# Attention with a two-layer FFN on one core: which score tile goes first after a row-maximum block, and a plan made anew

## The chip, the cores and the metric

The kernel runs on one core of one Trainium2 chip. Its time is the device time of one execution in microseconds (us); lower is better. The kernel before took 840.44 us, the median of three runs (839.09 to 842.27). Three engines matter most here: TensorE (PE in the profile; PEld are its weight loads), VectorE (DVE) and ScalarE (ACT); GpSimd (POOL) adds, and SyncE (SP) issues transfers.

## The reference

Attention over 32 heads (4 x 8) with pairs of queries averaged, so 576 queries and 1152 keys of depth 64 per head; then an FFN on 2304 tokens of width 512, with an inner width of 2048:

```python
q_pool = q.reshape(B, H, S // 2, 2, D).mean(axis=3)
scores = scale * np.matmul(q_pool, k.transpose(0, 1, 3, 2))
scores = scores - np.max(scores, axis=-1, keepdims=True)
attn = np.exp(scores)
attn = attn / (np.sum(attn, axis=-1, keepdims=True) + 1e-09)
x = np.matmul(attn, v)                      # then heads side by side: 2304 x 512
h = x @ w_in
g = np.maximum(h, 0.0) + alpha * np.minimum(h, 0.0)
return g @ w_out
```

## The kernel before

The heads are worked on in 16 pairs. The two heads of a pair lie in the two 64-row halves of TensorE's array (`both`, line 635): head 0 of a pair is tile 0, head 1 tile 1. A matmul on one tile can run beside one on the other.

Three kinds of work of a pair go to the tiles. **Row maxima** (`pair_max`, line 792): q against k, 128 queries by 384 keys in one matmul (line 818), into one PSUM bank, and VectorE reduces the bank to a maximum per query (line 839). A pair has 24 such blocks and 4 short ones for the last 64 queries (two matmuls of line 825 each). The list runs through the tiles in turn, 0, 1, 0, 1. The maxima are turned (line 855) and stored as `mq`. **Scores** (`half_main`, line 934): for each half of the queries (288) and each of 9 blocks of 128 keys, eight matmuls, four for each tile: high by high, high by low and low by high parts of k and q, and a product that takes off the maximum. They are issued 0, 1, 0, 1, ... into two banks, one for each tile. ACT takes the exponential of each bank (line 968). **Weighted sums** (line 995): after nine blocks of a half, the exponentials against v, in both tiles' columns, all rows; no score or maximum runs beside them. Sums of the exponentials (lines 981 and 1017), the division and the store to DRAM follow in `pair_end`.

The FFN (`hidden`, `low_sweep`, `high_sweep`, all through line 479) uses weights that VectorE and ACT split into parts (`w_convert`, lines 399 to 438: lines 409, 415, 421, 427 and 391 on VectorE). Ten conversions have no later use than attention's end and are spread over it; the rest come later.

The order of all instructions is made when the program is built, by a planner (`Scheduler`, line 109). Each piece of work is given to `add` with its engine, a planned duration in ns, what it reads and writes, and a priority in units of heads. `run` steps through a planned time: on each engine it looks at what could start within a slack of the earliest start (SLP, SLA, SLD for TensorE, ACT, VectorE) and takes the lowest priority number. Planned durations are constants: 545 for a score block, 130 for a maximum block, 190 for a short one. PSUM banks are handed out by the planner as well: `share` (line 1104) gives lists of banks to scores, maxima and the FFN, EARLY first and LATE from the end of head 13 (SWITCH) on, and a taker gets the one that is planned to be free first. The parameters of `attention_ffn` are priorities, slacks and lists of this kind. Engines then run their queues in the planned order and wait for each other by semaphores.

Of the kernel before, what the change touches and what calls it, by code (L numbers as in the profile page):

```python
# [13 lines left out]
AF = mybir.ActivationFunctionType  # L14
# [94 lines left out]
class Scheduler:  # L109
# [3 lines left out]
    def __init__(self, col_cost, turn, to_pe, from_pe, slack, dma_fixed):  # L113
        self.tasks, self.ready = [], [[] for _ in range(5)]
        self.free = [0.0] * 5
        self.dma_free = 0.0
        self.now = 0.0
        self.col = 0
        self.lock_free = 0.0
        self.turn = turn  # L120
        self.col_cost, self.to_pe, self.from_pe, self.slack = col_cost, to_pe, from_pe, slack
        self.dma_fixed = dma_fixed
        self.hold = ()

    def add(self, eng, dur, emit, reads=(), writes=(), uses=(), deps=(), prio=0.0, col=0, size=0, kind=None, dma=False, lock=False, fixed=None):
        t = Task()
# [99 lines left out]
def attention_ffn(  # L226
# [8 lines left out]
    NLO: int = 5,  # L235
    PB: int = 13,
    QB: int = 2,
    DF: int = 1985,
    D0: int = 1153.836,
    AQ: int = 0,  # L240
    F0: float = 7.572,
    F2: float = 0.839,
    FD: tuple = (1, 1, 1),
    WE: float = 24.0,
    WG: int = 1,
    WT: float = 6.74,
    WM: int = 2,
    WB: int = 300,
    WN: int = 2,
    TO_PE: int = 89,  # L250
    FROM_PE: int = 40,
    SLP: int = 45,
    SLA: int = 48,
    SLD: int = 138,
    QL: float = -0.025,
    KL: float = 1.207,
    KR: float = 1.497,
    KS: float = 0.082,
    M0: float = 1.211,
    E0: float = 1.868,  # L260
    BD: int = 7,
    SD: tuple = (3, 20),
    LD: tuple = (0, 33),
    TD: tuple = (3, 33),
    SR: float = 0.311,
    KQ: float = 0.342,
    KKB: int = 2,
    FQ: int = 1,
    FB: tuple = (1, 7),
    SF: int = -39,  # L270
    Q0: float = -2.2,
    Q1: float = 2.605,
    GROUPS: tuple = ((8,), (8,)),
    PARTS: tuple = (((0, 1, 2), (3, 4), (5, 6), (7, 8)), ((0, 1, 2, 3), (4, 5, 6, 7, 8))),
    JH: int = 0,
    AB: int = 10,
    ADDS: tuple = ((4, 6, 8), (6, 8)),
    PL: int = 0,
    LV: int = -2,
    LW: int = -8,  # L280
    GSB: int = 1,
    YSB: int = 4,
    R0: float = 4.187,
    R1: float = -5.36,
    R2: float = -7.727,
    R3: float = -0.231,
    W0: float = 5.34,
    W1: float = 1.69,
    W2: float = 18.088,
    W3: float = 0.137,  # L290
    YL: float = 0.337,
    MS: float = 0.136,
    EARLY: tuple = ((1, 2, 3, 4, 6), (0, 5, 6), ()),
    LATE: tuple = ((0, 1, 2, 3, 4, 5, 6), (0, 1, 2, 3, 4, 5, 6), (1, 2, 3, 4, 5, 6)),
    SWITCH: int = 13,
    GL: float = 23.364,
    COL: float = 0.151,
    HW: float = -1.194,
    XB: int = 4,
    PT: int = 17,  # L300
    VB: int = 4,
# [4 lines left out]
    QA: float = 1.0,  # L306
    REUSE: int = 6,
    NW: tuple = (464, 460, 460, 460, 460),
    RP: float = 31.088,
    RS: float = -1.017,  # L310
    RM: int = 30,
    RATE: float = 342.662,
):
    nc = tc.nc
# [6 lines left out]
    HQ = SQ // 2  # L321
# [6 lines left out]
    SCALE = 0.5 / float(D) ** 0.5  # L328
# [20 lines left out]
    sch = Scheduler(COL, SF, TO_PE, FROM_PE, (SLP, SLA, SLD, 0, 0), DF)  # L349
# [285 lines left out]
    both = [slice(i * D, (i + 1) * D) for i in range(2)]  # L635
# [156 lines left out]
    def pair_max(n, w):  # L792
# [15 lines left out]
        for x, (t, j, i) in enumerate(items):  # L808
            ms, d = Buf(r_ms), both[i]
            p = n - M0 - 0.5 * MS * (len(items) - 1 - x)  # L810
            if first:
                p = -9 + 0.01 * x
            rest = t < 0
            m = S // 4 if rest else JW

            def rows(t=t, j=j, d=d, ms=ms):
                if t >= 0:
                    nc.tensor.matmul(  # L818
                        out=ms.t[:, :JW], lhsT=w.q1.t[d, starts[t]:starts[t] + P],
                        rhs=w.k1.t[d, j * JW:(j + 1) * JW], start=True, stop=True,  # L820
                    )
                    return
                for u in range(2):
                    c = (2 * j + u) * (S // 4)
                    nc.tensor.matmul(  # L825
                        out=ms.t[:, :S // 4], lhsT=w.rt.t[d, D - D * u:D - D * u + P],
                        rhs=w.k1.t[d, c:c + S // 4], start=u == 0, stop=u == 1,
                    )

            dur = 190 if rest else 130  # L830
            if first:
                deps = w.k_in if rest else [w.k_in[j], w.q_in[2 * (t > 1)]]
                add(PE, dur, rows, uses=[w.q1, w.k1], reads=[w.rt] if rest else (), deps=deps, writes=[ms], prio=p, kind="m", col=1)
# [19 lines left out]
        def turn():  # L853
# [9 lines left out]
            for i, d in enumerate(both)  # L863
# [4 lines left out]
                out=mm.t[:2, :D], in0=mt.t[1][:2, :D], in1=mm.t[:2, :D].bitcast(F32), op=ALU.max  # L868
# [65 lines left out]
    def half_main(n, h, w):  # L934
# [7 lines left out]
        for c in range(NC):  # L942
            s = slice(c * P, (c + 1) * P)
            p, ps = Buf(r_p), Buf(r_ps)
            at = n + h + c / NC

            def scores(ps=ps, s=s):
                pairs = ((w.k1, w.q1), (w.k1, w.q2), (w.k2, w.q1), (None, w.mq))
                for x, (k, r) in enumerate(pairs):
                    for i, d in enumerate(both):  # L950
                        nc.tensor.matmul(  # L951
                            out=ps.t[i][:, :HQ], lhsT=k.t[d, s] if k else neg[d], rhs=r.t[d, q],
                            start=x == 0, stop=x == len(pairs) - 1,
                        )
# [10 lines left out]
            for i in range(2):  # L965
                add(
                    ACT, act(HQ, True),
                    lambda ps=ps, p=p, i=i: nc.scalar.activation(  # L968
                        out=p.t[:, i], in_=ps.t[i][:, :HQ], func=AF.Exp, scale=SCALE
                    ),  # L970
                    reads=[ps], writes=[p], prio=at + 0.01 * i,
                )
# [261 lines left out]
```

## Time and profile before

| what | value |
|---|---|
| median of three runs | 840.44 us (839.09 to 842.27) |
| profiled execution | 839.95 us, of which the span 838.2 us |
| PE busy | 825.2 us (98%) |
| PEld busy | 691.4 us (82%) |
| DVE busy | 567.0 us (68%) |
| ACT busy | 437.4 us (52%) |
| POOL busy | 262.4 us (31%) |

The profile is of one execution. The span goes from the first instruction to the last. Busy times are of instructions in flight, so a tile of TensorE can stand still while the engine counts as busy. "out<-in" names the tiles that an instruction writes and reads: `bank` is a PSUM bank, `pa` the exponentials, `bx` the maxima of a block. Attention fills the time up to about 440 us, with FFN work beside it from about 385 us on; the rest is the FFN.

### The profile page before, as it was taken

To read this page: it belongs to the slowest core of one execution; us is meant where nothing else is said; L and a number is where in the kernel's file an instruction comes from. 1 tells how busy PE (TensorE), PEld (TensorE's weight loads), DVE (VectorE), ACT (ScalarE), POOL (GpSimd) and SP (SyncE) were. 2 spreads that over 40 slices of the span, in tenths; PEclk is the share of its full clock that TensorE was granted. 3 is DMA by queue.
4 is the path that set the end of the run, shared out by engine and by line. 5 is a ranking of instruction groups with operands and counts; after the bars stand their busy time and mean duration, and the time that the engine had idled before them with its cause. 6 is when DMAs were issued, how large, how long until landed. Compare 5 with 4: busy or idle time off the path is not lost.

```text
span 838.2 us, 17447 instructions
## 1 busy us (share of the span) xinstructions
PE 825.2 (98%) x6690; PEld 691.4 (82%) x6690; DVE 567.0 (68%) x1035; ACT 437.4 (52%) x1124; POOL 262.4 (31%) x196
## 2 busy tenths in 40 slices
PE   8999999999999999999999999999999999999997
PEld 8767777676777777776779999998898988988986
DVE  7999999999998988889963799632242232322422
ACT  4657676675766676665754676643232233332321
POOL 5665665565565665654550000000000000000000
PEclk9999999999999999999999999999999999999999
DMA  8234345634354433323233768581330421300301
GB/s 274 58 89 164 82 144 140 197 115 123 87 179 122 122 116 77 83 72 109 69 124 121 248 195 260 177 228 58 91 92 3 120 59 46 91 0 1 91 1 45
DMA packets 67759, 93.71 MB, mean 112 GB/s; under 512 B 20004, under 2 KB 45404, under 8 KB 67676
## 3 DMA queue, kind: packets, MB, share of 16 engines
q1 hardware_dynamic: 65516, 88.18, 33.9%
q0 software_dynamic: 2160, 4.42, 3.6%
q8 instruction: 52, 0.85, 0.4%
q14 instruction: 31, 0.25, 0.1%
HBM read 73.48 MB, written 19.02 MB: 110 GB/s over the span
## 4 chain that ended last, share of the span: by engine, by line
PE 86%; DVE 9%; DMA 2%; issue 1%; ACT 1%; SPq 0%; DVEq 0%; ACTq 0%
PE bank L479 44%; PE bank L951 18%; PE bank L995 15%; PE bank L818 6%; DVE bx L839 3%; PE bank L1017 2%; DMA wraw<-wt 1%; DVE x L1066 1%; DVE pa L981 1%; PE bank L825 1%; PE bank L1129 1%; DMA kk<-kt 1%; DVE pos L515 1%; DVE r L1054 0%; DVE wbits L415 0%
## 5 line engine op out<-in xcount | busy, mean ns | idle before, releaser
L981 POOL TENSOR_TENSOR pa<-pa,pa 128x576 f32<-128x576 f32 x160 | 240.5, 1520 | 155.9 <-ACT pa L968 104.4
L839 DVE TENSOR_REDUCE bx<-bank 128x1 f32<-128x384 f32 (+1 forms) x448 | 214.0, 533 | 22.5 <-PE bank L818 19.9
L968 ACT ACTIVATE pa<-bank 128x288 f32<-128x288 f32 x576 | 199.7, 417 | 25.9 <-PE bank L951 17.4
L951 PE MATMUL bank<-q,k 64*128 64x288 f32 x1728 | 206.2, 311 | 0.8 <-DVE mq L923 0.6
L951 PEld LDWEIGHTS bank<-q,k 64*128 64x128 f32 x1728 | 163.3, 184 | 21.1 <-issue 9.3
L995 PE MATMUL bank<-pa,vv 128*64 128x288 f32 x1152 | 146.8, 409 | 0.0
L995 PEld LDWEIGHTS bank<-pa,vv 128*64 128x64 f32 x1152 | 79.9, 137 | 54.8 <-issue 3.8
L526 DVE TENSOR_TENSOR gw<-gs,gw 128x460 fp32r<-128x460 f32 (+1 forms) x55 | 35.1, 638 | 121.2 <-ACT gw L521 121.2
L951 PE MATMUL bank<-mq,neg 64*128 64x288 f32 x576 | 115.2, 291 | 0.0
L818 PE MATMUL bank<-k,q 64*128 64x384 f32 x384 | 110.1, 362 | 3.5 <-DVE bx L839 2.0
L521 ACT ACTIVATE gw<-gs 128x460 fp32r<-128x460 f32 (+1 forms) x55 | 32.4, 589 | 126.7 <-PE bank L479 115.2
L479 PE MATMUL bank<-wlow,wh 128*128 128x460 f32 (+1 forms) x320 | 93.0, 371 | 0.0
L479 PE MATMUL bank<-gw,wh 128*128 128x460 f32 (+1 forms) x320 | 92.8, 371 | 0.0
L951 PEld LDWEIGHTS bank<-mq,neg 64*128 64x128 f32 x576 | 83.3, 184 | 0.0
L818 PEld LDWEIGHTS bank<-k,q 64*128 64x128 f32 x384 | 62.4, 185 | 16.2 <-DVE bx L839 10.0
L515 DVE SCALAR_TENSOR_TENSOR gs<-gs,nal 128x460 f32<-128x460 f32 (+1 forms) x55 | 38.4, 699 | 52.9 <-ACT gs L510 52.9
L479 PE MATMUL bank<-x,wlow 128*128 128x288 f32 x480 | 66.3, 296 | 0.0
L479 PEld LDWEIGHTS bank<-wlow,wh 128*128 128x128 f32 x320 | 60.0, 188 | 7.1
L479 PE MATMUL bank<-gs,wlow 128*128 128x288 f32 x480 | 65.8, 295 | 0.1
L479 PEld LDWEIGHTS bank<-gw,wh 128*128 128x128 f32 x320 | 60.1, 188 | 6.8
L479 PEld LDWEIGHTS bank<-x,wlow 128*128 128x128 f32 x480 | 64.2, 188 | 1.6 <-issue 1.4
L479 PEld LDWEIGHTS bank<-gs,wlow 128*128 128x128 f32 x480 | 63.9, 188 | 1.4 <-DVE gs L526 0.5
(90 smaller groups left out, 1006.2 us busy)
## 6 DMA issues: line engine op xcount, KB each, us to landing
wraw<-wt SPq DMA_DIRECT2D x32, 512.0 KB
vv<-vt SPq DMA_DIRECT2D x32, 288.0 KB
xs<-x SPq DMA_DIRECT2D x32, 288.0 KB
x<-xs SPq DMA_DIRECT2D x32, 288.0 KB
kk<-kt SPq DMA_DIRECT2D x15, 576.0 KB
r<-rrd SPq DMA_DIRECT2D x64, 72.0 KB
yp<-ys SPq DMA_DIRECT2D x32, 144.0 KB
wlow<-xs SPq DMA_DIRECT2D x16, 288.0 KB
```

The source lines that it names most:

```text
L479: nc.tensor.matmul(out=ps[:, :n], lhsT=w[a, c // DMO][:, c % DMO:c % DMO + P], rhs=lo(hl), start=(first and i == 0), stop=(last and i == 2),)
L515: lambda: nc.vector.scalar_tensor_tensor(out=flat(pos), in0=flat(neg), scalar=nal[:, f:f + 1], in1=flat(pos), op0=ALU.mult, op1=ALU.add),
L521: ACT, act(n), lambda: nc.scalar.activation(out=gs.t[:, 0, :n], in_=flat(pos), func=AF.Copy),
L526: lambda: nc.vector.tensor_tensor(out=gs.t[:, 1, :n], in0=flat(pos), in1=gs.t[:, 0, :n].bitcast(F32), op=ALU.subtract),
L818: nc.tensor.matmul(out=ms.t[:, :JW], lhsT=w.q1.t[d, starts[t]:starts[t] + P], rhs=w.k1.t[d, j * JW:(j + 1) * JW], start=True, stop=True,)
L825: nc.tensor.matmul(out=ms.t[:, :S // 4], lhsT=w.rt.t[d, D - D * u:D - D * u + P], rhs=w.k1.t[d, c:c + S // 4], start=u == 0, stop=u == 1,)
L839: nc.vector.tensor_reduce(out=bx.t[:, at, j:j + 1], in_=ms.t[:, :m], axis=AX.X, op=ALU.max)
L951: nc.tensor.matmul(out=ps.t[i][:, :HQ], lhsT=k.t[d, s] if k else neg[d], rhs=r.t[d, q], start=x == 0, stop=x == len(pairs) - 1,)
L968: lambda ps=ps, p=p, i=i: nc.scalar.activation(out=p.t[:, i], in_=ps.t[i][:, :HQ], func=AF.Exp, scale=SCALE),
L981: lambda a=a, b=p, part=part, e=e: e.tensor_tensor(out=part.t, in0=a.t, in1=b.t, op=ALU.add),
L995: nc.tensor.matmul(out=av.t[i * D:(i + 1) * D, :HQ], lhsT=w.vv[i].t[:, e], rhs=p.t[:, i], start=(e == 0), stop=(e == NC - 1),)
L1017: nc.tensor.matmul(out=ps.t[g * 32:(g + 1) * 32, :HQ], lhsT=ones, rhs=acc[n + g // 2][j].t[:, g % 2], start=j == 0, stop=j == m - 1, tile_ ...
```

## The change

The planner keeps in `sch.tile` the tile of the last block that was issued. A scores block looks at it when it is issued: if the last one ended on tile 0, the block issues tile 1 first, else tile 0 first, and notes the tile that it issues last. The two exponentials of the block follow in that order. Besides, the planned times of maximum blocks become 165 and 108 ns, and the parameters of the plan are set anew.

```diff
         self.hold = ()
+        self.tile = 1
...
-    TO_PE: int = 89,
+    TO_PE: int = 88,
     FROM_PE: int = 40,
-    SLP: int = 45,
-    SLA: int = 48,
+    SLP: int = 39,
+    SLA: int = 78,
...
-    KL: float = 1.207,
-    KR: float = 1.497,
-    KS: float = 0.082,
-    M0: float = 1.211,
+    KL: float = 1.242,
+    KR: float = 2.229,
+    KS: float = 0.067,
+    M0: float = 1.209,
...
-    LD: tuple = (0, 33),
+    LD: tuple = (1, 33),
...
-    SR: float = 0.311,
+    SR: float = 0.906,
...
-    SF: int = -39,
-    Q0: float = -2.2,
+    SF: int = -33,
+    Q0: float = -2.408,
...
-    ADDS: tuple = ((4, 6, 8), (6, 8)),
+    ADDS: tuple = ((2, 4, 6, 8), (6, 8)),
...
-    LW: int = -8,
+    LW: int = -5,
...
-    R1: float = -5.36,
-    R2: float = -7.727,
+    R1: float = -5.889,
+    R2: float = -4.86,
...
-    W2: float = 18.088,
+    W2: float = 16.818,
...
-    EARLY: tuple = ((1, 2, 3, 4, 6), (0, 5, 6), ()),
-    LATE: tuple = ((0, 1, 2, 3, 4, 5, 6), (0, 1, 2, 3, 4, 5, 6), (1, 2, 3, 4, 5, 6)),
+    EARLY: tuple = ((1, 2, 3, 4, 5), (0, 5, 6), ()),
+    LATE: tuple = ((0, 1, 2, 3, 4, 5, 6), (0, 5, 6), (3, 4, 5, 6)),
...
-    HW: float = -1.194,
+    HW: float = -0.27,
...
-    RP: float = 31.088,
-    RS: float = -1.017,
+    RP: float = 31.836,
+    RS: float = -2.623,
...
-            def rows(t=t, j=j, d=d, ms=ms):
+            def rows(t=t, j=j, d=d, ms=ms, i=i):
+                sch.tile = i
...
-            dur = 190 if rest else 130
+            dur = 165 if rest else 108
...
-            def scores(ps=ps, s=s):
+            order = []
+
+            def scores(ps=ps, s=s, order=order):
                 pairs = ((w.k1, w.q1), (w.k1, w.q2), (w.k2, w.q1), (None, w.mq))
+                order.extend((1, 0) if sch.tile == 0 else (0, 1))
+                sch.tile = order[1]
                 for x, (k, r) in enumerate(pairs):
-                    for i, d in enumerate(both):
+                    for i in order:
+                        d = both[i]
...
-                    lambda ps=ps, p=p, i=i: nc.scalar.activation(
-                        out=p.t[:, i], in_=ps.t[i][:, :HQ], func=AF.Exp, scale=SCALE
+                    lambda ps=ps, p=p, o=order, i=i: nc.scalar.activation(
+                        out=p.t[:, o[i]], in_=ps.t[o[i]][:, :HQ], func=AF.Exp, scale=SCALE
```

## Rows read from the trace of the kernel before

**Rows 1.** The page: busy times of all engines, and PE's busy tenths by slice.
```profile
PE 825.2 (98%) x6690; PEld 691.4 (82%) x6690; DVE 567.0 (68%) x1035; ACT 437.4 (52%) x1124; POOL 262.4 (31%) x196
...
PE   8999999999999999999999999999999999999997
```

**Rows 2.** The chain in order of time: start us, length us, what, instructions.
```profile
58.17 4.52 PE bank L995 x36
...
240.16 4.52 PE bank L995 x36
...
265.32 4.52 PE bank L995 x36
...
339.95 4.52 PE bank L995 x36
352.62 4.52 PE bank L995 x36
...
490.59 5.34 DMA wraw<-wt
501.22 331.19 PE bank L479 x1733
```

**Rows 3.** Busy time by stretch: length, PE, PEld, DVE, ACT, POOL, granted clock, DMA.
```profile
50.00:100.00 50.00, 49.12 (x518) 37.71 (x517) 48.41 (x96) 33.84 (x94) 32.37 (x22) 1.00 0.33 96
...
300.00:350.00 50.00, 50.00 (x539) 37.97 (x537) 42.47 (x84) 32.84 (x93) 30.43 (x23) 1.00 0.39 109
```

**Rows 4.** PE by line, 344.5 to 352.6 us: operation, tiles, shapes, count, busy, mean.
```profile
L951 PE MATMUL bank<-q,k 64*128 64x288 f32 x60 | 7.0, 308 | 0.0
L951 PE MATMUL bank<-mq,neg 64*128 64x288 f32 x20 | 4.1, 291 | 0.0
L818 PE MATMUL bank<-k,q 64*128 64x384 f32 x12 | 3.3, 360 | 0.0
L825 PE MATMUL bank<-k,rt 64*128 64x288 f32 x8 | 1.2, 296 | 0.0
```

**Rows 5.** Timeline of PE up to 309.24 us: start, length, line, count.
```profile
309.10 0.29 PE L951 MATMUL bank<-mq,neg 64*128 64x288 f32 x2
309.23 0.34 PE L818 MATMUL bank<-k,q 64*128 64x384 f32 x1
309.23 0.29 PE L951 MATMUL bank<-q,k 64*128 64x288 f32 x1
```

**Rows 6.** Lines 818 and 825, 290.3 to 309.235 us: count, ns min/median/max, first and last start.
```profile
L818 PE MATMUL bank<-k,q x13: 327/335/441, 295.8 to 309.2; 64*128 64x384 f32 x13
...
L825 PE MATMUL bank<-k,rt x8: 289/292/332, 300.5 to 301.8; 64*128 64x288 f32 x8
```

**Rows 7.** Timeline of ACT, 310.19 to 310.92 us.
```profile
310.19 0.41 ACT L968 ACTIVATE pa<-bank 128x288 f32<-128x288 f32 x1
...
310.50 0.41 ACT L968 ACTIVATE pa<-bank 128x288 f32<-128x288 f32 x1
```

**Rows 8.** Timeline of PE's weight loads, 310.65 to 310.965 us.
```profile
310.65 0.18 PEld L951 LDWEIGHTS bank<-q,k 64*128 64x128 f32 x1
...
310.96 0.19 PEld L951 LDWEIGHTS bank<-q,k 64*128 64x128 f32 x2
```

**Rows 9.** Waits: who for whom, us in total, times, longest us.
```profile
ACT pa L968 <- PE bank L951: 17.4, 68, 0.7
```

**Rows 10.** Line 409, 30 to 240 us: count, ns min/median/max, first and last start.
```profile
L409 DVE TENSOR_SCALAR wbits<-wraw x10: 407/412/766, 34.4 to 218.9; 128x512 int32<-128x512 int32 x10
```

**Rows 11.** DVE by line, whole span.
```profile
L427 DVE SCALAR_TENSOR_TENSOR wmag<-wmag,wbits 128x512 f32<-128x512 f32 x32 | 24.3, 766 | 0.7 <-ACT wmag L406 0.3
```

**Rows 12.** Waits from 50 to 240 us.
```profile
PEld bank L818 <- DVE bx L839: 6.4, 20, 1.0
```

**Rows 13.** Waits from 258 to 385 us.
```profile
PEld bank L818 <- DVE bx L839: 1.0, 5, 0.2
```

**Rows 14.** Timeline of ACT, 339 to 352 us: in brackets the idle time before it.
```profile
344.46 0.26 ACT L680 ACTIVATE rt<-qs 128x64 fp32r<-128x64 f32 x1 [3.94 <-DMA qs<-qt]
```

More of the change, by code (lines that the diff above doesn't have):

```diff
@@ L237, in attention_ffn @@
     QB: int = 2,
-    DF: int = 1985,
+    DF: int = 2010,
     D0: int = 1153.836,
     AQ: int = 0,
-    F0: float = 7.572,
+    F0: float = 7.519,
     F2: float = 0.839,
     FD: tuple = (1, 1, 1),
-    WE: float = 24.0,
+    WE: float = 24.18,
     WG: int = 1,
-    WT: float = 6.74,
+    WT: float = 5.439,
     WM: int = 2,
@@ L288, in attention_ffn @@
     W1: float = 1.69,
-    W2: float = 18.088,
+    W2: float = 16.818,
     W3: float = 0.137,
-    YL: float = 0.337,
-    MS: float = 0.136,
-    EARLY: tuple = ((1, 2, 3, 4, 6), (0, 5, 6), ()),
-    LATE: tuple = ((0, 1, 2, 3, 4, 5, 6), (0, 1, 2, 3, 4, 5, 6), (1, 2, 3, 4, 5, 6)),
+    YL: float = 0.326,
+    MS: float = 0.134,
+    EARLY: tuple = ((1, 2, 3, 4, 5), (0, 5, 6), ()),
+    LATE: tuple = ((0, 1, 2, 3, 4, 5, 6), (0, 5, 6), (3, 4, 5, 6)),
     SWITCH: int = 13,
```

## The prediction

> **What bounds the kernel now.** I read the shares of the engines first, then the chain of work that ended last in order of time, then stretches of 50 us, then the inside of one stretch. TensorE is busy for 825.2 of 838.2 us, and between the first slice and the last none is below nine tenths [rows 1]. The chain's last piece is the FFN's line 479, 331.19 us without a break from 501.22 us on [rows 2]: neither the order of two score tiles nor a priority in attention can shorten that. So the change acts in attention, up to about 440 us, and there the profile has two stages. From 50 to 100 us VectorE is busy for 48.41 us of 50 and TensorE has small gaps; from 300 us on VectorE has fallen to 42.47 and TensorE shows none, both at the full granted clock [rows 3]. In the chain the weighted sums (line 995) come once per half of a head pair. From 58.17 to 240.16 us are seven pairs, 26.0 us each; from 265.32 to 339.95 three, 24.88 us each [rows 2]. The reader is to see that the early pairs, where VectorE is full, take 1.12 us more each, 7.9 us in all, and that the late ones are paced by something else.
>
> What paces a late pair is inside a busy TensorE. Between the sums that end at 344.47 us and those at 352.62 there are 80 score matmuls, 12 long blocks of row maxima and 8 matmuls of the short blocks [rows 2, 4]. Two 64-row tiles run side by side. On one tile a 288-column matmul follows the last after 0.13 us (309.10 to 309.23 in [rows 5]); a 384-column block, by its columns, takes an estimated 0.18. One tile then has 44 x 0.133 + 6 x 0.18 = 6.9 us of work in a stretch of 8.15. The lost 1.2 us are what a better order could win here; with the other half, which holds fewer blocks, I put a pair at an estimated 2 us.
>
> **The change part by part.** *The order of the tiles.* No matmul is added or removed. Each scores block issues the same eight matmuls, but tile 1 ahead of tile 0 where the block before it ended on tile 0; the two exponentials follow in the same order. The thought is that after a maximum block on tile 0 the first score matmul waits behind it and holds up the one for tile 1. The rows contradict this. The block at 309.23 is the 17th of its pair (13 matmuls of line 818 and 8 of line 825, two of these to a block, [rows 6]); blocks alternate between the tiles and begin with 0, so it ran on tile 0. In the program the score matmul of tile 0 comes next, and that of tile 1 only behind it. Yet a score matmul starts in the same hundredth as the block [rows 5]: it can only be tile 1's, which passed its neighbour. The tile that the change would serve first is already served first.
>
> The Trainium skill, "TensorE: Matmul & The Clock Gate", section "Part 3: Packing small matmuls — row/col tiling", says otherwise: matmuls start and end strictly in program order. This case's trace doesn't agree, by the two starts at 309.23 in [rows 5]. By that rule the change would pay; the sum would be that of the third rival below.
>
> What does hold both tiles is a wait for a PSUM bank. Scores alternate between pairs of banks, and a block may start on a bank only when the exponentials of the block two earlier have read it. These run one after the other: those of one block start at 310.19 and 310.50, and the second ends at 310.91 [rows 7]. The weight loads show the effect: the scores' first load goes at 310.65 and their next only at 310.96, when two go together, 0.05 us behind the second exponential [rows 8]. So while the second bank is awaited, only the first tile's first matmul runs. Now let the order be reversed against the block two earlier: the first load needs the bank that comes free last, and even that one matmul, 0.133 us, isn't done in the wait. That is the price of a reversed block where the exponentials set the pace; with the same order as two blocks earlier the price is nothing. A pair has 18 score blocks, ten in the half of [rows 4] (80 matmuls by 8) and eight in the other; the first two of a half find banks long free, so 14 remain. If half are reversed, 7 x 0.133 = 0.93 us a pair, 14 us over 15 pairs; in seven early pairs VectorE's wait covers it, which leaves 7 to 8 us.
>
> The bound below nothing is the time that ACT waits for scores in all, 17.4 us in 68 waits [rows 9]; a better order could at most halve it, about -9. I take the order alone as 0, by the nearest row (in [rows 5] tile 1 is already ahead), and keep -9 and +8.
>
> *The plan made anew.* Planned block times fall from 190 and 130 ns to 165 and 108, and some 35 priorities, slacks and bank lists move. Planned times run on no engine; they change the order in which the queues are written, and through that who waits for whom. The work per engine stays, so the change can win only waits: the 7.9 us of the early pairs and about 2 us in each late one.
>
> The early pairs carry VectorE's work on FFN weights: ten conversions between 34.4 and 218.9 us [rows 10], each one instruction of 0.41 us (the median there) and four like line 427's 0.766 [rows 11], so 3.5 us, 35 us where VectorE has no time to spare. All ten already lie there, so nothing more can be put in; moving two beyond 240 us would win up to 7 us. The new W2 makes the second five more urgent by 1.27 heads, which speaks against that. I take that a quarter of the 7.9 us goes, -2.0, and keep -8 to +6, the upper end being as many waits made elsewhere.
>
> The bank lists: from head 13 on, maxima get three banks instead of seven. With three, weight loads of line 818 waited for VectorE 6.4 us in 20 waits early [rows 12]; with seven, 1.0 us in 5 late [rows 13]. So the price is between 0 and 5.4 us. The late stage has VectorE time to spare, so I take 0. (Early scores trade bank 6 for 5, both shared with maxima already: nothing.)
>
> KR makes ACT's conversions of the next pair's q and k more urgent by 0.73 heads. Now ACT waits 3.94 us for q's load until 344.46 us [rows 14], with the copy of the sums and the next exponentials queued behind it, and the weighted sums on TensorE cover the wait, since they run to 344.47 [rows 2]. With that cover gone, 3.9 us fall on the scores. The loads of q and k move by 0.03 to 0.21 heads on SP's queue, past loads for V, and that of q's second half on POOL's not at all: nothing. The six reused weight conversions (RP, RS) and the later ones (HW) move among VectorE work from 390 us on; there a weight load stands in the chain for 5.34 us [rows 2], while TensorE has FFN work, so 0, with -1 to +5. What ADDS, LD, SR, R1, R2 and LW set is not reached in this program or cut off at the same value: nothing.
>
> **Rivals.** *Same (likeliest).* Order 0, plan -2.0. The profiled execution took 839.95 us (838.2 of span, 1.75 around), 0.49 under the median 840.44. So 839.95 - 2.0 = 837.95 for such an execution, 838.4 for the median.
>
> *The plan wins the early stage.* Early pairs fall from 26.0 to 25.3 us, 7 x 0.7 = 4.9, and eight late ones by 0.25 each, 2.0: 840.4 - 6.9 = 833.5. For it: 1.12 us a pair is plain waiting. Against it: VectorE's load there doesn't change.
>
> *Order counts after all, as if in program order.* Then each score block behind a tile-0 block holds tile 1 for the block's 0.18 us, half of which counts, since the other tile works: 7 x 0.09 x 15 pairs = 9.4, so 831. Against it: [rows 5].
>
> *Slower: reversed blocks wait for the later bank.* 840.4 + 7 = 847, and 845.5 with the plan's gain. The order turns with the number of maximum blocks in between, so a block is reversed against the one two earlier when the two gaps hold an odd number together, and the case decides from about half of the blocks reversed. A pair has 28 maximum blocks (24 long, 4 short) for 16 gaps, so one and two in turn, sum three, is natural; two and two would avoid it, and shorter planned blocks may lead there. *Other waits of the new plan* (3.9 and 5.4 above) would end near 845 as well.
>
> *It doesn't do what it says:* with two blocks in every gap the order would stay as it is; that lies within the first case.
>
> **How the numbers follow.** Chances: same 0.38, plan wins 0.28, program order 0.06, reversed blocks 0.18, other waits 0.10. A measurement of this kernel can tell about 0.5% (4.2 us) from no change, so up to 836.2 is faster and from 844.6 slower: faster 0.34, same 0.38, slower 0.28. The likeliest case alone spans 836.2 to 844.6. Eight in ten take in most of either side: 830 to 848.
>
> **What would show it.** *Order worth nothing:* late pairs still 24.9 us from sum to sum of line 995, and a score matmul starting with a tile-0 block, as now. *Reversed blocks:* late pairs at 25.4 or more, ACT waiting for scores longer than 17.4 us, and loads of both tiles held behind the later exponential. *Plan:* early pairs under 25.5 us, weight conversions later than 218.9 us. *Banks:* line 818 waiting for VectorE late for more than 1.0 us. The prediction is wrong if late pairs fall below 24.3 us, since it has no mechanism for that, or if anything moves behind 501 us.

## The result and the profile after

The changed kernel took 846.72 us (median of six runs, 845.39 to 849.16) beside 840.23 us for the kernel before (six runs): a ratio of 1.0078, 95% interval 1.0059 to 1.0096. It is slower by 6.6 us, where I had forecast 2 us less. Below, "+6.6 us" means such a ratio less one, times 840.4. The profiled execution took 846.4 us, its span 844.6.

The page of the changed kernel (busy times; PE's busy tenths in 40 slices; share of the chain by engine):

```profile
span 844.6 us, 17378 instructions
...
PE 826.6 (98%) x6704; PEld 687.2 (81%) x6704; DVE 570.3 (68%) x1035; ACT 438.0 (52%) x1124; POOL 268.9 (32%) x196
...
PE   8999999999999999999999999999999999999997
...
PE 80%; DVE 14%; ACT 2%; issue 1%; DMA 1%; POOL 1%; DVEq 0%; POOLq 0%; ACTq 0%
```

Against [rows 1] nothing has moved: TensorE is busy 1.4 us longer, no slice shows a hole. Only the chain tells more: VectorE has 14% of it, before 9%. The loss is found with the weighted sums as milestones. Chain of the changed kernel in order of time (start us, length us, what; line 995 is now 1002, line 479 is 480):

```profile
30.56 4.53 PE bank L1002 x36
...
256.87 1.78 PE bank L480 x12
...
274.03 4.52 PE bank L1002 x36
...
373.98 4.52 PE bank L1002 x36
...
440.71 4.52 PE bank L1002 x36
...
452.04 386.79 PE bank L480 x2160
```

And three more pieces of the chain before:

```profile
31.23 4.58 PE bank L995 x36
...
364.81 4.52 PE bank L995 x36
...
432.69 4.52 PE bank L995 x36
```

With 265.32 from [rows 2] and the spans:

| stretch | before us | after us | difference |
|---|---|---|---|
| start to first sum | 31.23 | 30.56 | -0.7 |
| nine early pairs | 234.09 (26.0 each) | 243.47 (27.1 each) | +9.4 |
| four late pairs | 99.49 (24.9 each) | 99.95 (25.0 each) | +0.5 |
| to the last sum | 67.88 | 66.73 | -1.2 |
| to the end | 405.5 | 403.9 | -1.6 |

So the whole loss lies in the early pairs, the stage where VectorE is full [rows 3]. Of the 9.4 us, 1.8 are twelve FFN matmuls at 256.87, work that came forward from the end; the kernel before had its first at about 389 us. The other 7.6 are lost in waits. Busy time by stretch, first 25 to 275 us of the kernel before (length, PE, PEld, DVE, ACT, POOL, granted clock, DMA):

```profile
25.00:275.00 250.00, 246.42 (x2557) 184.71 (x2556) 238.75 (x454) 164.52 (x460) 152.28 (x106) 1.00 0.43 124
```

and after, the same stretch, two of [rows 3], and a short one:

```profile
50.00:100.00 50.00, 46.43 (x488) 33.93 (x486) 48.94 (x90) 31.59 (x90) 28.45 (x21) 1.00 0.31 91
...
242.00:245.40 3.40, 3.40 (x30) 3.40 (x30) 2.61 (x8) 2.14 (x6) 2.75 (x2) 0.50 0.19 66
...
300.00:350.00 50.00, 49.95 (x536) 37.28 (x534) 42.78 (x83) 32.69 (x92) 30.36 (x23) 1.00 0.39 109
...
25.00:275.00 250.00, 242.10 (x2492) 177.45 (x2490) 235.96 (x444) 162.16 (x452) 153.89 (x103) 0.99 0.42 122
```

TensorE stands still 4.3 us longer (busy for 242.10 in place of 246.42) and starts 65 matmuls fewer, though twelve of its matmuls are the FFN's. So 77 of attention's are missing, at the 10.4 a us of the kernel before an estimated 7.4 us: the standing still and, for the rest, tiles that wait while the engine counts as busy. The largest hole, in TensorE's timeline (in brackets the idle time and who ended it), then VectorE's and GpSimd's:

```profile
238.15 0.33 PE L820 MATMUL bank<-k,q 64*128 64x384 f32 x1
240.22 0.44 PE L820 MATMUL bank<-k,q 64*128 64x384 f32 x1 [1.74 <-DVE bx L841]
```

```profile
235.90 0.76 DVE L410 TENSOR_SCALAR wbits<-wraw 128x512 int32<-128x512 int32 x2
236.57 2.53 DVE L416 SCALAR_TENSOR_TENSOR wbits<-wraw,wbits 128x512 int32<-128x512 int32 x2
239.02 0.68 DVE L422 SCALAR_TENSOR_TENSOR wbits<-wraw,wbits 128x512 int32<-128x512 int32 x1
239.62 3.33 DVE L841 TENSOR_REDUCE bx<-bank 128x1 f32<-128x384 f32 x7
```

```profile
237.11 1.44 POOL L988 TENSOR_TENSOR pa<-pa,pa 128x576 f32<-128x576 f32 x1 [2.44 <-ACT pa L975]
```

Two weight conversions lie together ahead of the reductions that free the maxima's banks, and the second instruction of line 416 lasts 1.92 of the 2.53 us, beside an add of GpSimd. (The kernel before has two conversions together as well, twice: at 88.5 and at 218.6 us.) From 242.0 to 245.4 us the granted clock is then 0.50 (the lower of its two levels, 1.2 GHz). By the counts above that is 30 matmuls where the late stage has 36 in as long: an estimated 0.6 us, less than the hole itself. Waits, who for whom (us in total, times, longest), after:

```profile
ACT pa L975 <- PE bank L958: 36.3, 108, 2.0
...
PEld bank L820 <- DVE bx L841: 18.0, 51, 2.0
...
PEld bank L958 <- ACT pa L975: 9.4, 33, 1.5
```

and the last two of the kernel before (the first is [rows 9], 17.4):

```profile
PEld bank L818 <- DVE bx L839: 10.0, 36, 1.0
...
PEld bank L951 <- ACT pa L968: 1.8, 6, 0.6
```

All three have grown: ACT waits for scores twice as long, maxima wait for VectorE 8 us more, and scores wait for exponentials five times as long, the sign of reversed blocks. Which of these costs the 6.6 us the profile alone doesn't tell.

### The profile page after: what moved, and what is told of

It reads as the page before. It is cut to its first block, busy times and chain, and to the rows that moved or that the text cites. A ratio compares the mean times of both kernels' runs of the same rounds, so it can differ in the third digit from the quotient of the medians.

```text
span 844.6 us, 17378 instructions
## 1 busy us (share of the span) xinstructions
PE 826.6 (98%) x6704; PEld 687.2 (81%) x6704; DVE 570.3 (68%) x1035; ACT 438.0 (52%) x1124; POOL 268.9 (32%) x196
## 4 chain that ended last, share of the span: by engine, by line
PE 80%; DVE 14%; ACT 2%; issue 1%; DMA 1%; POOL 1%; DVEq 0%; POOLq 0%; ACTq 0%
PE bank L480 47%; PE bank L958 14%; PE bank L1002 11%; PE bank L820 5%; DVE bx L841 4%; DVE pa L988 2%; DVE x L1073 2%; DVE wbits L416 1%; ACT pa L975 1%; DVE k L700 1%; PE bank L1024 1%; DMA qs<-qt 1%; DVE r L1061 1%; DVE wbits L410 1%; PE bank L827 1%
## 5 line engine op out<-in xcount | busy, mean ns | idle before, releaser
L988 POOL TENSOR_TENSOR pa<-pa,pa 128x576 f32<-128x576 f32 x160 | 248.4, 1583 | 150.5 <-ACT pa L975 106.7
L841 DVE TENSOR_REDUCE bx<-bank 128x1 f32<-128x384 f32 (+1 forms) x448 | 213.8, 534 | 17.4 <-PE bank L820 14.5
L958 PE MATMUL bank<-q,k 64*128 64x288 f32 x1728 | 197.2, 310 | 2.6 <-ACT pa L975 1.6
L958 PEld LDWEIGHTS bank<-q,k 64*128 64x128 f32 x1728 | 147.9, 186 | 22.3 <-ACT pa L975 9.4
L820 PE MATMUL bank<-k,q 64*128 64x384 f32 x384 | 113.2, 371 | 7.6 <-DVE bx L841 6.6
L958 PE MATMUL bank<-mq,neg 64*128 64x288 f32 x576 | 104.7, 293 | 0.0
L820 PEld LDWEIGHTS bank<-k,q 64*128 64x128 f32 x384 | 61.9, 186 | 28.1 <-DVE bx L841 18.0
L958 PEld LDWEIGHTS bank<-mq,neg 64*128 64x128 f32 x576 | 73.3, 186 | 0.0
```

The lines of the kernel that those rows point to most:

```text
L820: nc.tensor.matmul(out=ms.t[:, :JW], lhsT=w.q1.t[d, starts[t]:starts[t] + P], rhs=w.k1.t[d, j * JW:(j + 1) * JW], start=True, stop=True,)
L841: nc.vector.tensor_reduce(out=bx.t[:, at, j:j + 1], in_=ms.t[:, :m], axis=AX.X, op=ALU.max)
L958: nc.tensor.matmul(out=ps.t[i][:, :HQ], lhsT=k.t[d, s] if k else neg[d], rhs=r.t[d, q], start=x == 0, stop=x == len(pairs) - 1,)
L988: lambda a=a, b=p, part=part, e=e: e.tensor_tensor(out=part.t, in0=a.t, in1=b.t, op=ALU.add),
```

## The experiments

All are timed against the kernel before. A block is called reversed when its tile order differs from that of the last block on the same pair of banks, counted in the program's order.

### The plan alone, the order alone

*Plan alone*: the changed kernel with a fixed order.

```diff
-                order.extend((1, 0) if sch.tile == 0 else (0, 1))
+                order.extend((0, 1))
```

> The changed plan, with the scores issued tile 0 first in every block as before; nothing else differs from the changed kernel, and the planned order of every queue is the same but for the two tiles of a score block. If reversed blocks cost the time (155 of 288 score blocks in the changed kernel go the other way round than the block that last used their pair of banks, here none): 840 us, within 2 of the kernel before. If the new plan costs it (bank lists, priorities): 846 to 847, as the changed kernel.

Measured 846.13 us, ratio 1.0067 [1.0050, 1.0085]: +5.6 us. Early pairs lengthen, late ones stay at 24.9. The plan costs all but about 1 us.

The early pairs aren't all alike in the two kernels. The first three take 3.6 us more than before in the plan alone and 3.5 in the changed kernel. The eighth, with the hole at 238 us, takes 29.0 us in the changed kernel but 26.4 here (before 25.4). VectorE's conversions, GpSimd's add, the hole and the stretch behind it, here:

```profile
236.59 1.29 DVE L416 SCALAR_TENSOR_TENSOR wbits<-wraw,wbits 128x512 int32<-128x512 int32 x2
```

```profile
237.12 2.62 POOL L988 TENSOR_TENSOR pa<-pa,pa 128x576 f32<-128x576 f32 x1 [2.44 <-ACT pa L975]
```

```profile
239.00 0.44 PE L820 MATMUL bank<-k,q 64*128 64x384 f32 x1 [0.50 <-DVE bx L841]
```

```profile
242.00:245.40 3.40, 3.40 (x41) 2.62 (x39) 3.40 (x10) 2.46 (x9) 2.25 (x3) 1.00 0.03 1
```

The same two conversions meet the same add, within 0.02 us of the times in the changed kernel; but here the add lasts longer (2.62 in place of 1.44 us) and line 416 doesn't, the hole is 0.50 us, and the clock stays. So the plan costs its 5.6 us without the large hole.

*Order alone*: the new rule with before's planned times and parameters.

```diff
...
-    SLP: int = 39,
-    SLA: int = 78,
+    SLP: int = 45,
+    SLA: int = 48,
...
-            dur = 165 if rest else 108
+            dur = 190 if rest else 130
```

> The plan of the kernel before with the new rule for the order of the tiles alone; 172 of 288 score blocks are reversed against the last user of their banks. If reversed blocks cost the time: 846 to 848 us, late pairs at 25.3 us or more, ACT's wait for scores over 30 us (17.4 before). If the plan costs it: 840. If matmuls kept program order on the two tiles: faster than before, some 832.

Measured 848.42 us, 1.0090 [1.0074, 1.0105]: +7.6 us, with 172 of 288 score blocks reversed. Chain and waits of this kernel:

```profile
34.26 4.54 PE bank L1002 x36
...
272.82 4.52 PE bank L1002 x36
...
375.28 4.52 PE bank L1002 x36
```

```profile
ACT pa L975 <- PE bank L958: 30.2, 102, 0.7
...
PEld bank L958 <- ACT pa L975: 15.3, 55, 1.0
```

Between the last two of these sums lie four late pairs, 25.6 us each: 0.7 us more than before, 3.0 in all. Between the first two lie the nine early pairs, 238.56 us: 4.5 more than before, 0.5 a pair. Scores wait 15.3 us for exponentials, before 1.8. These are the signs that the prediction set for reversed blocks; that the early pairs lose as well it didn't have.

*Every block reversed*, and *tile 1 always first* (none reversed, but 137 blocks start on the tile just used, before 109), both on before's plan, shown against the order alone:

```diff
-                order.extend((1, 0) if sch.tile == 0 else (0, 1))
+                banks = tuple(id(x) for x in ps.t)
+                sch.seen = getattr(sch, 'seen', {})
+                order.extend(sch.seen.get(banks, (1, 0))[::-1])
+                sch.seen[banks] = tuple(order)
```

```diff
-                order.extend((1, 0) if sch.tile == 0 else (0, 1))
+                order.extend((1, 0))
```

> The plan of the kernel before; every score block goes the other way round than the last user of its pair of banks (273 of 288), whatever maximum block came before it, so 131 blocks start on the tile just used. If a reversed block costs some 0.13 us wherever the exponentials set the pace: slower than the order alone, 849 to 852 us. If what costs is something else in the new rule (the exponentials' order, a switch of tile after maxima): no clear relation to the count, 840 to 846.

> The plan of the kernel before; every score block issues tile 1 first and its exponential first, so none is reversed, while 137 blocks start on the tile just used (109 before). If only the reversal costs: 840 us, within 2 of before. If the tile just used costs: slower by a quarter of what the other rule would win; if tile 1 first is bad in itself: over 843.

The first: 848.76 us, 1.0092 [1.0075, 1.0108], 273 reversed, late pairs 25.6 again. The second: 842.81 us, 1.0027 [1.0016, 1.0038]; scores wait 2.2 us for exponentials. So it is chiefly the reversal that costs. Tile 1 first, with more starts on the tile just used, costs 2.3 us, which is clear of noise; which of its two differences does that isn't shown. Nor does the price grow with the count, though I had expected it to (849 to 852 us): 172 and 273 reversed blocks cost the same.

*Every block reversed on the new plan*: the edit of the first in the changed kernel.

```diff
-                order.extend((1, 0) if sch.tile == 0 else (0, 1))
+                banks = tuple(id(x) for x in ps.t)
+                sch.seen = getattr(sch, 'seen', {})
+                order.extend(sch.seen.get(banks, (1, 0))[::-1])
+                sch.seen[banks] = tuple(order)
```

> The changed plan with every score block issued the other way round than the last user of its banks (277 of 288 reversed; 155 in the changed kernel, none in the run of the plan alone). If on this plan the exponentials are through before the bank is needed, because maximum blocks waiting for VectorE set the pace: 845 to 848 us, as with 155 and with none. If a reversed block costs here as on the old plan: 850 and more, late pairs 25.4 us and over.

Measured 848.55 us, 1.0084 [1.0062, 1.0106]: with 277 reversed only 1.4 us over the plan alone, within both intervals. Waits from 275 to 385 us, in the order alone and then in the changed kernel:

```profile
PEld bank L958 <- ACT pa L975: 5.4, 22, 0.3
```

```profile
PEld bank L958 <- ACT pa L975: 2.0, 9, 0.3
```

With about as many reversed blocks (172 and 155) the later bank is waited for 22 times on the old plan and 9 times on the new one. The reversal's price belongs to the plan that it meets. What in the new plan gives the exponentials the time isn't settled.

### Which part of the plan

The kernel before, with its order, and one group of the new plan in each: the planned times of maxima; the bank lists; TO_PE, the slacks, the cost of a change of kind (SF) and the planned time of a transfer (DF); all other changed parameters.

```diff
-            dur = 190 if rest else 130
+            dur = 165 if rest else 108
```

```diff
-    EARLY: tuple = ((1, 2, 3, 4, 6), (0, 5, 6), ()),
-    LATE: tuple = ((0, 1, 2, 3, 4, 5, 6), (0, 1, 2, 3, 4, 5, 6), (1, 2, 3, 4, 5, 6)),
+    EARLY: tuple = ((1, 2, 3, 4, 5), (0, 5, 6), ()),
+    LATE: tuple = ((0, 1, 2, 3, 4, 5, 6), (0, 5, 6), (3, 4, 5, 6)),
```

```diff
-    DF: int = 1985,
+    DF: int = 2010,
...
-    TO_PE: int = 89,
+    TO_PE: int = 88,
...
-    SLP: int = 45,
-    SLA: int = 48,
+    SLP: int = 39,
+    SLA: int = 78,
...
-    SF: int = -39,
+    SF: int = -33,
```

```diff
...
-    KL: float = 1.207,
-    KR: float = 1.497,
+    KL: float = 1.242,
+    KR: float = 2.229,
...
-    W2: float = 18.088,
+    W2: float = 16.818,
...
-    HW: float = -1.194,
+    HW: float = -0.27,
...
```

> The kernel before with the planned times of maximum blocks alone changed, 165 and 108 ns for 190 and 130. Tile order as before. In the changed plan maximum blocks wait more for VectorE (weight loads of the maximum blocks: 17.0 us in 51 waits with the changed plan and the old tile order, 10.0 in 36 before). If planned times that are too short put maximum blocks too early in TensorE's queue, this part alone costs: 844 to 847 us and more than 13 us of such waits. If another part of the plan costs, 840 to 842.

> The kernel before with the lists of PSUM banks alone changed (early scores 5 for 6; late maxima three banks for seven, late FFN four for six). If three banks for the maxima are what costs, the loss is in the late stage: 844 to 847 us, late pairs over 25.2 us, maximum blocks waiting for VectorE late for 3 us and more (1.0 before). If not: 840 to 842.

> The kernel before with the planner's model of the chip alone changed: slacks of TensorE and ACT (45 and 48 ns to 39 and 78), delay to TensorE, cost of a change of kind, fixed time of a transfer. If ACT's wider slack lets other work pass exponentials, ACT and TensorE lose time to each other: 843 to 846 us. If the slack is small beside ACT's own pieces (0.41 us): 840 to 842.

> The kernel before with the priorities alone changed (loads and conversions of q and k, maxima, weight conversions and others); bank lists, planned times, slacks and tile order as before. If the priorities cost (conversions of q and k that go ahead of exponentials, weight conversions that go in a bunch): 843 to 847 us, most of it in early pairs. If not: 840 to 842.

Measured 1.0109 [1.0090, 1.0128], 1.0075 [1.0053, 1.0096], 1.0042 [1.0027, 1.0058] and 1.0112 [1.0091, 1.0133]. Their sum is 3.4%, five times what they cost together, and no group is free. These parts have no prices that add up: each makes another order of the queues. Three of them lose in the early pairs, with late ones at 24.7 to 24.9; the bank lists lose from 240 to 326 us, in pairs of 28.2, 30.2 and 28.1 us, where 36 FFN matmuls that came forward fill 5.7 us and are paid back behind. In the third, most of the loss is in one pair of 31.2 us (before 25.4; the pair ahead of it is 2.4 us shorter). Its timeline and stretch:

```profile
237.15 1.15 PE L818 MATMUL bank<-k,q 64*128 64x384 f32 x2 [2.21 <-DVE bx L839]
```

```profile
236.00:244.00 8.00, 6.85 (x54) 6.56 (x54) 6.29 (x14) 3.19 (x10) 2.85 (x3) 0.57 0.41 98
```

A hole behind VectorE, with the granted clock near its lower level behind it, as in the changed kernel.

### Plans with no meaning

If any new order of the queues does this, edits without a meaning must do it too: planned times of maxima 1 ns shorter, 1 ns longer, and longer by as much as the change makes them shorter (215 and 152); and ACT's planned times 1 ns longer.

```diff
-            dur = 190 if rest else 130
+            dur = 189 if rest else 129
```

```diff
-            dur = 190 if rest else 130
+            dur = 191 if rest else 131
```

```diff
-            dur = 190 if rest else 130
+            dur = 215 if rest else 152
```

```diff
-        return n / 1.2 + (50 if psum else 93)
+        return n / 1.2 + (51 if psum else 94)
```

> The kernel before with the planned times of maximum blocks 1 ns shorter (189 and 129). A change without meaning, but the plan comes out in another order from about a sixth of TensorE's queue on. If what costs is that the kernel before has a plan picked among many, and any plan made anew is an ordinary one: 843 to 848 us, with one or two pairs of the early stage at 28 us or more. If the cost lies in what a parameter means (blocks planned too short): 840 to 841.

> The kernel before with the planned times of maximum blocks 1 ns longer (191 and 131); the order differs almost from the start. Any plan made anew: 843 to 848 us. If the meaning of a parameter counts: 840 to 841.

> The kernel before with planned times of maximum blocks 22 and 25 ns longer, the mirror image of the change. If short planned times cost because blocks are put too early in TensorE's queue (849.4 us with 165 and 108), longer ones cost nothing or win: 838 to 841. If any plan made anew costs: 844 to 850 as well.

> The kernel before with every planned time of ACT 1 ns longer. No block time, bank list, slack or priority is touched. Any plan made anew: 843 to 848 us, the loss again in single early pairs and none in late ones (24.8 to 25.0 us a pair). If the meaning of a parameter counts: 840 to 841.

All are slower, two of them (857.8 and 859.8 us) by more than I had expected of any plan made anew. With the rest of the plans tried:

| plan | ratio, interval | us | VectorE standing, us |
|---|---|---|---|
| before | 1 | 0 | 23.5 |
| slacks | 1.0042 [1.0027, 1.0058] | +3.5 | 25.1 |
| new plan, old order | 1.0067 [1.0050, 1.0085] | +5.6 | 25.8 |
| changed kernel | 1.0078 [1.0059, 1.0096] | +6.6 | 26.7 |
| bank lists | 1.0075 [1.0053, 1.0096] | +6.3 | 27.1 |
| 1 ns longer | 1.0095 [1.0061, 1.0128] | +8.0 | 29.6 |
| ACT 1 ns longer | 1.0106 [1.0084, 1.0127] | +8.9 | 30.6 |
| planned times 165, 108 | 1.0109 [1.0090, 1.0128] | +9.2 | 29.1 |
| other parameters | 1.0112 [1.0091, 1.0133] | +9.4 | 30.6 |
| 1 ns shorter | 1.0198 [1.0181, 1.0215] | +16.6 | 30.8 |
| 215, 152 | 1.0231 [1.0202, 1.0260] | +19.4 | 32.9 |

The last column is counted in the traces: of all VectorE instructions but reductions from 25 to 280 us, the time above the shortest of the same form, summed. It rises with the time in the main, by 9.4 us where the time rises by 19.4, so it is a sign and not the whole loss; the order alone has 25.3 at +7.6 us. What stands behind it is best seen in the kernel with 1 ns less. TensorE, VectorE and GpSimd around its largest hole:

```profile
207.79 0.33 PE L818 MATMUL bank<-k,q 64*128 64x384 f32 x1
213.20 0.68 PE L818 MATMUL bank<-k,q 64*128 64x384 f32 x1 [5.08 <-DVE bx L839]
```

```profile
204.83 0.44 DVE L1054 TENSOR_TENSOR r<-avs,r 128x288 f32<-128x288 f32 x1
205.20 3.80 DVE L1066 TENSOR_TENSOR x<-r,x 128x288 fp32r<-128x288 f32 x1
208.93 2.55 DVE L699 TENSOR_TENSOR k<-kk,k 128x1152 fp32r<-128x1152 f32 x1
211.40 0.44 DVE L1066 TENSOR_TENSOR x<-r,x 128x288 fp32r<-128x288 f32 x1
...
212.70 1.84 DVE L839 TENSOR_REDUCE bx<-bank 128x1 f32<-128x288 f32 x4
```

```profile
205.60 4.65 POOL L981 TENSOR_TENSOR pa<-pa,pa 128x576 f32<-128x576 f32 x3
```

Line 1066 takes 3.80 us where the same instruction takes 0.44 at 211.40, and line 699 takes 2.55 where 1.35 is usual (below). Together they stand 3.36 + 1.20 = 4.56 us, and GpSimd's three adds beside them take 4.65. The reductions, which TensorE waits for, come behind.

### Two causes taken away

*VectorE's weight conversions cut short*, queues in the same order: in before, in the changed kernel, and in the one with 1 ns less. Four steps of each of the ten leave out 448 of 512 columns, so those weights are not computed in full; the first step is shown, the other three are cut in the same way.

```diff
+        cw = 64 if f < NLO else DMO
...
-                out=bits.t, in0=raw.t[:, :, 1], scalar1=3, scalar2=0x3FFFFFF8,
+                out=bits.t[:, :cw], in0=raw.t[:, :cw, 1], scalar1=3, scalar2=0x3FFFFFF8,
...
```

> The kernel before, queue order kept, with the four VectorE steps that build the bits of the first ten FFN weight tiles done on 64 of 512 columns, so those weights are wrong; some 2.2 us of VectorE less for each, 22 us in all. If the early pairs are paced by VectorE: they fall from 26.0 to about 25.0 us and the time to 832 to 835. If something else paces them: 838 to 841.

> The changed kernel with the same cut (the first ten FFN weight tiles built on 64 of 512 columns). If the changed plan loses by pile-ups on VectorE: it falls by more than the kernel before does, to 833 to 837, within 3 us of that kernel with the cut. If it loses otherwise: it stays 5 to 7 us behind it.

> The plan made with times 1 ns shorter (857.8 us) with the same cut. If pile-ups on VectorE and the half clock behind them are its loss: it falls by 15 us or more, to 834 to 842, and the waits of 2 to 5 us on TensorE at 208 and 245 us go. If not: it stays over 850.

Measured 0.9964 [0.9952, 0.9976], 0.9989 [0.9975, 1.0003] and 1.0183 [1.0156, 1.0209]. Before wins 3.0 us, the changed kernel 7.5, and what lies between them falls from 6.6 to 2.1 us; the hole at 238 us and its slow stretch are gone. So about two thirds of the changed kernel's loss go with this work, and not at 236 us alone: its first three pairs are 1.9 us longer than those of the kernel before with the same cut, where they were 3.5 longer. Before itself wins less than I had expected of a stage paced by VectorE (832 to 835 us). The kernel with 1 ns less wins 1.3 us, within the intervals: its holes have another cause.

*GpSimd's adds cut short* (36 of 288 columns, so the sums of the exponentials leave out the rest), in before and in the one with 1 ns less:

```diff
-                    lambda a=a, b=p, part=part, e=e: e.tensor_tensor(out=part.t, in0=a.t, in1=b.t, op=ALU.add),
+                    lambda a=a, b=p, part=part, e=e: pair_sum(e, part, a, b),
```

```diff
...
+    def pair_sum(e, part, a, b):
+        n = HQ if e is nc.vector else 36
...
+        e.tensor_tensor(out=part.t[:, :, :n], in0=a.t[:, :, :n], in1=b.t[:, :, :n], op=ALU.add)
```

> The kernel before, queue order kept, with GpSimd's adds of the exponentials (line 981) done on 36 of 288 columns, so the sums of the exponentials are wrong. If VectorE's instructions stand while these adds run and the early pairs lose by that: 832 to 837 us, early pairs about 25.0 us. If not: 839 to 841.

> The plan made with planned times 1 ns shorter (857.8 us) with the same adds on 36 of 288 columns. If plans differ by how VectorE's instructions meet GpSimd's adds: within 4 us of the kernel before with the same cut, no VectorE instruction over 2 us, and the waits at 208 and 245 us gone. If plans differ in something else: 850 us or more.

Measured 0.9886 [0.9870, 0.9901] and 0.9966 [0.9952, 0.9981]. Before wins 9.6 us, the other 19.5, and the difference between the two plans falls from 16.6 to 6.7. VectorE by line, 30 to 275 us, of the kernel before (count, busy us, mean ns):

```profile
L1066 DVE TENSOR_TENSOR x<-r,x 128x288 fp32r<-128x288 f32 x16 | 17.2, 1101 | 0.0
L699 DVE TENSOR_TENSOR k<-kk,k 128x1152 fp32r<-128x1152 f32 x9 | 12.1, 1345 | 0.0
```

and with short adds (line 1066 is there 1075):

```profile
L699 DVE TENSOR_TENSOR k<-kk,k 128x1152 fp32r<-128x1152 f32 x9 | 12.1, 1346 | 0.0
L1075 DVE TENSOR_TENSOR x<-r,x 128x288 fp32r<-128x288 f32 x18 | 8.7, 515 | 0.1
```

Even in the kernel before line 1066 stands for more than half of its time, and the adds let it go when they are short. The last column of the table falls from 23.5 to 6.8 us, and the nine early pairs from 26.0 to 25.3 us each: 0.7 of the 1.1 us that an early pair had over a late one went with these adds. In the kernel with 1 ns less TensorE's busy time, 25 to 275 us, with full and then with short adds:

```profile
25.00:275.00 250.00, 238.25 (x2390) 177.50 (x2389) 235.40 (x429) 154.29 (x431) 144.74 (x98) 0.97 0.40 115
```

```profile
25.00:275.00 250.00, 247.02 (x2580) 186.21 (x2579) 223.28 (x456) 165.49 (x464) 57.16 (x114) 1.00 0.42 122
```

TensorE gets 8.8 us back and the granted clock is 1.00 throughout. Short adds also hand their results on earlier, and the two effects were not tried apart. Nor were the adds cut short in the changed kernel: that GpSimd has a part in its loss is read from its trace alone. The 6.7 us that remain are more than the 4 us I had allowed; a hole of 1.66 us at 205 us stays, behind an exponential, and this part is open.

## Why the prediction was wrong

**The plan made anew** is the step that failed. I took a quarter of the early pairs' 7.9 us as won (-2.0); alone it cost 5.6. The place was right (early pairs, VectorE's queue, nothing in the late ones), the sign was not. I read the 1.12 us of waiting in an early pair as what an ordinary plan leaves, from which another plan might as well take. (The early pairs are nine by the table above, and they took some 10 us more than late ones.) Nine other plans, four of them with no aim, all came out 3.5 to 19.4 us slower: before's plan lies at one end of these ten, and the waits it leaves are few. My upper bound, "as many waits made elsewhere", +6, held for the change and is less than what 1 ns did (8.0 and 16.6). I also took VectorE's 48.41 busy us of 50 [rows 3] for work. From 25 to 280 us 23.5 us of its busy time are instructions that stand, and with short adds of GpSimd they are 6.8.

The sign to look for, conversions later than 218.9 us [rows 10], did come (the last two at 235.9 and 236.2 us). I had priced two that move beyond 240 us as a gain of up to 7 us; these still lie in the full stage, and their meeting with an add went with a hole of 1.74 us in the changed kernel and of 0.50 us in the plan alone. That the whole of this work costs more on the new plan is shown by its cut (7.5 us won, before 3.0); which of its pieces cost the plan alone its 5.6 us is not shown.

**The order as nothing** came out right for this pair of kernels by luck: on its own plan the order costs 6.6 - 5.6 = 1.0 us, which the intervals don't tell from nothing, and late pairs stay at 25.0. On before's plan, from which I had read it, it costs 7.6. That total is the price of reversed blocks that I worked out (7 to 8 us), and all three signs came: late pairs of 25.4 or more (25.6), ACT waiting longer than 17.4 us (30.2), loads held behind the exponentials (15.3 us in place of 1.8). But I had put it on eight late pairs, 0.93 us each, and nothing on the early ones; measured are 0.7 in a late pair, with more blocks reversed than I had taken, and 4.5 in the nine early ones. So the wait of that rival is there, its rule, so much for each reversed block, does not hold, and the total agrees in part by chance. The rival's 847 is near the result by chance as well, since the time went elsewhere.

**Order as if in program order** (831) is refuted as a forecast: the rule alone on the old plan is slower, and leading with the tile just used more often costs at most the 2.3 us of the always-first kernel. The reading of [rows 5], that the free tile passes its neighbour, stands for that block, but I took one block for all. With the program's order set beside the starts in the trace of the kernel before, the first score matmul behind a long block on tile 0 starts within 0.1 us of it in 27 of 105 cases, and 0.17 us behind it in the median; behind a long block on tile 1 the median is 0.00. So the free tile mostly waited with its neighbour. (Program order isn't strict for all that: a score matmul starts at 310.69 us, ahead of the block at 310.82 that comes before it in the program.) The rule didn't shorten that wait either: in the order alone the median behind tile 0 is 0.19 us.

**Other waits of the new plan** (near 845) is the rival nearest to what came, but neither of its two waits did. **Banks as nothing**: line 820's loads wait late 1.8 us in 9 times (275 to 385 us), [rows 13] had 1.0 in 5, so by this row the lists' direct price is about 1 us. Alone they cost 6.3, by re-planning, between 240 and 326 us. **KR as nothing**: ACT's wait for q's load falls from 10.7 us in three times to 2.1 in one (275 to 385 us), and late pairs don't lengthen. **Conversions from 390 us on**, -1 to +5: from the last sum to the end the kernel is 1.6 us shorter, a little below my bound, and about what the twelve FFN matmuls took that had come forward. **Nothing behind 501 us**: from 452.04 us TensorE runs its FFN matmuls 386.79 us without a break, so nothing there pays back what attention lost.

**The range**, 830 to 848, held the time because the slower rivals had moved its upper end; the likeliest case did not.

## What to carry to other kernels

Before a change that makes a static plan anew is priced, measure what an edit without meaning does (1 ns on a planned time: +8.0 and +16.6 us here); a gain or loss smaller than that can't be laid to a parameter. Keep the queues' order fixed to test one rule, and test it on more than one plan, as the order alone showed 7.6 us that all but vanished on another. Where two banks are freed one after the other, issue in the order in which they are freed: here the reverse cost between about 1 and 7.6 us.

## What the runs showed of the hardware

VectorE stood for about as long as GpSimd's adds ran: 4.56 us in two instructions beside adds of 4.65 us. The Trainium skill, "SBUF — State Buffer", section "Summary: rules for kernel authors", says that a VectorE instruction with two inputs in SBUF and a GpSimd instruction that reads SBUF exclude each other: the one issued second blocks until the first has finished. Lines 1066, 699 and 416 have two such inputs, and the traces agree on who contends. In the kernel before they mostly agree on who stands as well: of the 16 times that line 1066 runs between 25 and 280 us, it takes 1.65 to 1.67 us in the eight where an add had begun 0.14 to 0.29 us ahead of it, and 0.44 to 0.46 us in the five where an add began behind it, was within 0.15 us of its end, or didn't run. By the starts in the records they don't agree on how long and on who in two places. In the kernel with 1 ns less line 1066 begins at 205.20 us, GpSimd's adds at 205.60, 206.97 and 208.76 (ahead of them it issues a transfer, from 205.00 on), and line 1066 ends at 209.00, behind the second: it stood for more than one instruction. And in the plan alone the add at 237.12 us began 0.07 us ahead of line 416, yet it was the add that took longer (2.62 us); in the changed kernel, with the same 0.07 us, it was line 416.

A hole of 1.74 us was followed by 3.4 us at half the granted clock, one of 2.21 us by a clock of 0.57 in the 8 us from 236 us on, one of 1.66 us, in the kernel with 1 ns less and short adds, by no loss of clock. The length of the hole doesn't decide it. The new plan with every block reversed has a hole of the same length in the same place, and its granted clock stays at 1.00 (from 241.80 to 250 us):

```profile
241.83 0.44 PE L820 MATMUL bank<-k,q 64*128 64x384 f32 x1 [1.74 <-DVE bx L841]
```

In the kernel with 1 ns more a hole of 2.49 us that ends at 163.75 us is followed by a clock of 1.00 as well. What decides is not shown. The price is small beside the hole: an estimated 0.6 us for the first by the late stage's count, 0.9 by the 41 matmuls that the plan alone has in the same stretch.
